# Scores on either pair of TensorE tiles: K and Q kept a second time with exchanged partition halves

## The chip, the cores and the metric

The kernel runs on one core of one Trainium2 chip. Its time is device microseconds of that core; 947.76 us is the median of three runs before the change (947.38 to 948.65). The engines are TensorE (PE; weight loads are listed apart as PEld), VectorE (DVE), ScalarE (ACT), GpSimd (POOL) and SyncE (SP), which issues most transfers.

## The reference

The input x has 224 x 224 positions of 96 channels. Attention is taken in two directions: the first 48 channels of q, k and v in 28 horizontal stripes of 8 rows, the last 48 in 28 vertical stripes of 8 columns. A stripe has 1792 positions.

```python
qkv = jnp.einsum('bhwc,cd->bhwd', x, wqkv)
q, k, v = (qkv[..., :C].copy(), qkv[..., C:2 * C].copy(), qkv[..., 2 * C:].copy())
scale = C2 ** (-0.5)
qh = q[..., :C2].reshape(B * nh, sw * W, C2)
...
ah = _softmax(jnp.einsum('bqc,bkc->bqk', qh, kh) * scale, axis=-1)
oh = jnp.einsum('bqk,bkc->bqc', ah, vh).reshape(B, H, W, C2)
...
o = jnp.pad(oh, ((0, 0), (0, 0), (0, 0), (0, C2))) + jnp.pad(ov, ((0, 0), (0, 0), (0, 0), (C2, 0)))
return jnp.einsum('bhwc,cd->bhwd', o, wo)
```

The vertical stripes (qv, kv, vv, av, ov) go the same way after a transposition of the positions.

## The kernel before

**Stripe pairs.** The 56 stripes are worked on two at a time: 28 stripe pairs P, 14 of horizontal stripes and then 14 of vertical ones. One stripe of a pair lies on partitions 0 to 63, the other on 64 to 127; 48 channels and one extra row are used of each 64. The four 64x64 tiles of TensorE are used as two pairs. The *straight* pair (mode "q" in the code) takes partitions 0 to 63 to output partitions 0 to 63 and 64 to 127 to 64 to 127; the *exchanged* pair (mode "v") takes 0 to 63 to 64 to 127 and the other way round. A *step* is two matmuls, one for each stripe, on the two tiles of one pair; matmuls of the two pairs can run at the same time.

**Units.** The 1792 queries are cut in four chunks (512, 512, 512, 256) and the keys in 28 blocks of 64. A unit is two key blocks (four in the last chunk) by one chunk: two score halves, each one step of 512 columns or two of 256, each into a PSUM bank of its own. There are 984 units for ScalarE and 388 for VectorE and GpSimd.

- A ScalarE unit: two score halves (function qk, line 778; letters "a" in the order), one activation with Exp over both banks (line 824, "A"), two product steps with V (function pv, line 804, "c"), added up in the chunk's bank.
- A VectorE unit computes the exponential through integers: two score halves ("b"), two conversions from PSUM to int16 tiles I (line 844, "j"), then for two units at once two passes that make U and E from I (line 849, "U"; written "u" where VectorE does the pass in place of GpSimd), and three pairs of product steps for I, U and E ("d", "d", "D").

Scores run on the straight pair and products on the exchanged one, because K and Q are stored stripe by stripe and the product's inputs are as the scores left them. For the first four key blocks of a chunk (TURN = 2, "turned" units) it is the other way round. V is stored to match.

**Around the units.** For the next stripe pair, prep() makes K, Q and V by projections from x (lines 535 and 637), with evacuations on VectorE; K's column sums and a small matmul (line 602) take the mean out of Q. x comes by two steps of transfers on SP: blocks() copies two stripes side by side into a scratch array in DRAM (line 411, two transfers), and load() transposes them into SBUF (line 418, two transfers). fin() multiplies a finished chunk with wo (lines 691 and 725), divides by the sums of weights, keeps the horizontal part in Ph_sb and, for vertical stripes, adds both and stores the result (lines 749 and 760; 24 stores on SP for most vertical stripe pairs).

**What sets the order.** Nothing is decided on the chip. Each kind of operation stands in a stream named by a letter. The string SEQ, 11330 letters written out in the file, takes the streams' operations one by one; this fixes the order on every engine, and SP's order of transfers too. The string BANK gives each operation that needs a PSUM bank one of the eight. Work.run() walks both strings, adds to each operation's inputs what last used its bank, and Work.emit() writes waits on semaphores: one counter per engine, and for TensorE one per pair of tiles. An engine runs its list in order, so an operation that waits holds back all behind it.

**Buffers that matter here.** Eight PSUM banks; eight tiles PT for ScalarE's results; NY = 4 sets of I and U and NL = 2 of E; two of K, Q and V, by the parity of P.

Of the kernel before, what the change touches and what calls it, by code (L numbers as in the profile page):

```python
# [6 lines left out]
BF16 = mybir.dt.bfloat16  # L7
# [9 lines left out]
TURN = 2  # L17
# [6 lines left out]
def ndc(P, c):  # L24
# [4 lines left out]
    "HiIxIihIiHiIhiiiihIiHiiihxIiiiIhiIiixhhxhhxxhhihHhxihhHhhhhhexhHhhxefHfxHfeexeaaxefAaxeafAxeaaxcecbAaeaVccjbAa"  # L29
    "acjcbxdAcajacbdAjbcacajxbUAacacjfAeacacfAxuacacbedAjdcacxaeDAbecaceajDbAacjabUcjAbcacajbAajfaUccfAeccaeafAoaaU"  # L30
    "cecAgadradrfdAbdaeDXaDjdbkAfUadjacffAcbeacacXdjbAdakdadjdfddAdceaucacXfcAcaceabdcdADjXafaffbAaeDaDDDjcbAUcacaj"
    "cbcDAcjabaccjcbAaUdaodfDADjadadbedfAdfacjacUcfcbAaedaddfjdAadaegddVdcArcdracacfcAaDeaDUbDDdjbcAacacjcDbcAacjac"
    "UbccDAjabaddocAadaddjcdUbdADdjagaDDDrAcbrcacacjUbcAacacjgccAcraodardbdgAUadjaddbDrAjDagacrcfAcUrcarcacbdAeaDaD"
    "fDjDAbcaceadfdAjdadaddecUdbAdadjafcDcAXXDebacajcbcUAcajcacbccAjcfaadodffAdbkeUadaddgjADbDacarjcbcAacrackcUjbdA"
    "fcacaejdfdAdabeadfdfUAXjcfabacecdAXcdadjabDdDAjbcacaDjfDAcaceUacDccAbaoaDcjbAgadardUjfdfAdfadradDfeADacaeccbVc"
    "fAajcaccbecAacjacUdbdAajdadbdjbddADaDajDdUDAacDcacbcDcAjdbacacjdUbAcajdadbdAodaDaDdjcdAcUdadagcbcArDcracacDcjA"
    "bcUacajgccAraodardbdgAdajUdadfDrAgarDacecfAcacreacUcbAdardadfdjdAbDaDeaDfDAdjacacdecdUAbdadjaDbDcAXXajcacbccAj"
    "bkcaUcacjcccAfadoadfdfAadaedkdbUcgAjcbDaDajcfcAacraecrbcfUcAjdadadebdAadadjdbdcdAXcjaUbaDdjDDAXabaffjDfAcDeacU"
    "accDAbcacjacccbcAoadaUdfjdAagadedffdfAracracDfDAebaUacecfcAcaedajdbdAadjbdadVdcjdAcbDaDjaDbDAdcUjacacbcdAcjaca"
    "cbcDAcjacUabDoAadadjdgddAdcrabraUcdDjdADbaDajDcbcAacjacfcUcAcaecagccAoadrardggUADaraDrddfrAdbrdacacjbcAUacacef"  # L40
    "cDAjDaDaDbecfAcaceacDdjbkdAadkajdDbdAjaUabdddddAXXjcacacbcAcjbacaUcccjcAfadaodfDfAbDaedadUgdjAdbacacrjcbcAaDra"
    "DDfjUDbAadadejdfdAadeaddcdcAXUbacajbdcdAXcDjabaDcjAcbUacacjcfcfAacaccfcbAoaaUcegAdadrajdfdAdraDaDfefdfAUabaecf"
    "ccjAbcacaecfcAcaVjcacbdedAadjbdadjbdAdUDaDajDdDbAcacjacbcdAcjaUcabdcDjbADcadajdAbdaodaUcdcdjcAdadagcbDrADDraca"
    "UcDcjbAcacajccgcAoaadrdbrUdgAdadrajDfDAdragacecfUAcacreaccfdAraddadbedfAdacajcbDADeaDajbkdDdkAcjdaUdaDbDcAXXaj"
    "cacbccAjbcacaUcjcccAfadoadfdfAadaedbdUDfAjDbcacaejcbcAacajcgdbUdArdajdadfrdAaDeaDdbdDAXUDjdabaccjdcAXfafafcbec"
    "DAacUacjcbcDAcajbacccjcAbadUaodfDAdjadadfdfefAaDageUcbcAracraccfjcAacacebcVcfAjadaddbedAadjbdaUDdDjdADbDacjacb"
    "cAdcjacaUcdbDAcajcabDoAdadadjUgdAdDarDarcdcbAcdajbadcDUcAjgaaccrDcrbAacacjccAUaodadbggAjdadadrdbArDaDarcjfUcAc"
    "acradfdedAadacebcfdAdjacacdDeAUbdaDajDbdADdjaDabcDjAXXcbcUacajcfcAcaecacbccAjafakcUofAdfdaaeddbAgdajdaDbDkrcAr"
    "aUcadjfdbdAcaecjadfcAcaceaUcfdfAXfadeabdDDdAXjafaDdbedADacaUjcDcbAcacjacbcDAcjabacccjcUAbaadodfDffAjadaddfedAa"
    "ceacVDbcfAjcacacbecAacUjadbddjbdAagadjdddDAaDrUaDrDbcdAjcaacbccdAcjabaUcDjcDAbacajdbddAjadacUcbocdAdaadjDgDdAc"  # L50
    "argarcDUcDArcarcacbcAccjcadaodbUAaDjaDcfcdgAbedadacrcjbAUdadadrfddAjgaadeddcAdcUarcarbdcAdDjabaDDjAfDaDaeUfcDc"
    "AXXaceacbccAjbacaccjkcccAfkadoaUdffAdaedadgdbArDfarDaccUejbAcacacjbcfdAdjadadbedAacacjbfdfAXcfjabUacDedDAXdadj"
    "abDdDAjDcacUacbcAcDjacaccccAbaoadUdfdjAdfadaedfDfAaDeagcfUcrAbracacedfAdadaeddjbAcVacajcbccAjbacaccjbDUAddaacj"
    "dcDbADaDjacbcdAcjdUcabaoDADajbadgddAjadUaDdrDdrcAbadajdcbcADcjacUagDcArcbrcacaccjAcaadoUdfdAadeadDgbDArdajcacf"
    "UcrAcbdaedadfdAjdadagebDADaDrajbDAcracUacdjcdAbdadjabcDcAXXDjcacaUcbcAacjacfcccecAfaodadbkdfUAgdjadadfrbDAraDa"
    "ceccAakjacUbddfjdbAdacaecjfdAdaceaUcdDdAXbaDajbdDdDAXDjabaDcUjcbAcacajccffAcfcaeacccUAcboaaddfjDAagaDedffAdfUr"
    "dardacfcAeabacecfdAcaVjcacbceAadjbdaddjbAddacacjUdDDAaDbaDcjbcdAacjacbcdcUAjabacDcjDbAadaodcAcjbUadadgjcdADdad"
    "rabrDdcADcjaUgacDrcAbrcacaccjcAaoadUdbdfAjdadadeDgbADacracjUbccAracagjcfdAdardeadfUdAcracaddecdAbacajDdbdDAjaf"
    "aDeDDDAXXbcaucaccAjbcakcakcjcccAfaodaUdfdfADbaeDaddgjAdbDaDarjUDbDAacracfcjcbAcacaejcfcAbadeaUdDdDAXdjabadddjd"
    "cAXdadabucfAcfacjacfcAbecacacjccAcbaoadUdfcAjaDaDbedfAfadjadfUdbAecaaccfjcAcbeacagcjVAdadadbrdfrdAadaDeUdDjdDA"  # L60
    "bcacjaDcbAcdjacacbUccdAjabaccDjDbAadaodDUAdjbadaDdcjdAcgadarbcrdcADUcacjacbcADcjagaccrcAoaUdardbdgAjdadadbrcfA"
    "rDDajcaUgcAaecacfcrDrAbcacadefdAdajdabdedAdUDaDajDdbAdadjabcDcDAXXjcaUcacbcfAcjacacccecAfaodakdbUDfADfjadadebd"
    "AdgaacrcrckcAUajadfdddbeAacajcbdfdAjcacaDdeDUdAXbdDajbaDDcAXDjabadcjcbUAcacjacffAcfcaeacccAbcUoadadfjdAbadaedf"
    "fAdfjaDgaDecbAUacrjaddbdAracacfcjcAacacVefdcbAecadajdbcdUAcjdcacaDbDAaDjbDacdcjdAbUacajcDbDAaodaddjbgAdaUDarDj"
    "dcdAcdardabcDcAjDgacUacrcbrAacacjccbAcoadajUdbAgdajgaddrdAbrDaDarcjfUcAcacracfcAedadadfedAdUadeabdcdcAjdbaDaDj"
    "dDAafabcecAXXjDDDakcakcbucAacacjbcccccAjafUadodfdfAadaedgdbDArDarcaUcfjcbAcacaejcbdfAdjdadadefUdfAabaDdjDdDAXD"
    "faceabcdAXcDUjabaDcdjcbAacjaccfcAacUeaccccbAoadadfjDfAfabeadgdjAbVdadarDjbcAcacracfUcjAcbcacaeDfDAadeadjdbdUAa"
    "dajddcdcdAcacaDbDDcAjbUcacacjDcAdcabaoddAaDajDUgcDcrDAdrabaddcjbcAdadjaUbcdcAjgaaccrcbrAacacoUcAjadadbDfAjDada"
    "dedgUAbdacracjbccAracagjcfdADarDeaUDfDAdradadDedDAbadajcdUbdcAdjabadcjcAXXfcacaecbcAkcjbackacccjcAUfaadodffAad"
    "eaddgbdArDfarDacUcejbcAacacjbcfDAdjabadedUAadadjbfdfAXfjacacdcedcAXabadjcbcdAaDjaDDfcAuacaccDebDUAcacajbccAoad"  # L70
    "adfjfgAfadeaddfdrAVacracDbeDfAcacaedUdjAabdadjbddddAcjacacbcdDuAaDaDdjDbcAUacjacbccDAjacabcDjbAdaUdajdbdAcajca"
    "cbDAodDadadUjcdgcAacragrDcDcAacracrbcUcAjcccadaodbAdajdadgdfDrADragaUdebdAcacrajdbdAcracacfjcAbadeadUdDdDAjdba"
    "DaDjdcAfaafceDUcDAXXcaceacbcAacjacbccjkcccAafkadodfUdfAadaedgdbDArDarcacfjcbUAcadeajdbdfAdjdadacedcAbcacjabdDd"
    "AXDjabUaDdDjfAXcfafabecDAcDacjUaccbcAajcaccccbAoaaddUfjgAdadaedffdfAracracfDDeAbaUcaecfcAceacajcbdAadjbdadVdjb"
# [111 lines left out]
class Work:  # L186
# [29 lines left out]
    def run(s, seq, digits):  # L216
# [4 lines left out]
        for c in seq:  # L221
# [14 lines left out]
            if q != c:  # L236
                op.eng, op.fn = "dve", op.alt
# [697 lines left out]
```

## Time and profile before

| | |
|---|---|
| median of three runs | 947.76 us (947.38 to 948.65) |
| the profiled execution's own time | 947.77 us |
| its span | 945.7 us |
| granted TensorE clock | 0.997 of full |
| TensorE, at least one matmul running | 936.0 us |
| VectorE busy | 881.6 us |
| ScalarE busy | 925.2 us |
| GpSimd busy | 769.2 us |
| bytes moved by DMA | 57.09 MB |

The profile is of one execution. A matmul's end is modelled, and matmuls on different tiles overlap, so TensorE's busy time does not tell how full each pair of tiles is. A row of the timeline gives the start, the length, engine, line and operation, what is written and read, and how many instructions are merged in it. A row of the groups gives the number of instructions, their busy time and mean length, and then the engine's idle time just before them with what ended it. A row of the waits reads: who waited, for whom, the total in us, how often, and the longest. A row of the windows gives the stretch, its length, the busy time and number of instructions of PE, PEld, DVE, ACT and POOL, the clock, the DMA share and GB/s.

### The profile page before, as it was taken

How to read it: one execution, taken by the hardware profiler on the slowest of the kernel's cores; microseconds unless marked ns; L12 is line 12 of the kernel's file. 1: busy time of each engine (PE TensorE's matmuls, PEld its weight loads, DVE VectorE, ACT ScalarE, POOL GpSimd, SP SyncE). 2: the span in 40 equal slices, each digit the busy share in tenths (PEclk: the TensorE clock that was granted, in tenths of full speed). 3: DMA queues.
4: the chain of work that ended last, by engine and by line, in shares of the span. 5: the costliest groups of instructions: out<-in, count | busy, mean ns of one | idle time of the engine just before them, and what ended most of it. 6: DMA issues, size and time to landing. Idle time of an engine off the chain costs nothing.

```text
span 945.7 us, 48281 instructions
## 1 busy us (share of the span) xinstructions
PE 936.0 (99%) x21770; PEld 625.8 (66%) x21770; DVE 881.6 (93%) x1754; ACT 925.2 (98%) x993; POOL 769.2 (81%) x512
## 2 busy tenths in 40 slices
PE   9999999999999999999999999999999999999997
PEld 4666766676776677666666767766666666667664
DVE  8999999999999999999999999999999999999994
ACT  7999999999999999999999999999999999999996
POOL 3778988888886888787898888889879888878883
PEclk9999999999999999999999999999999999999998
DMA  8724513440441343244120515545533534461112
GB/s 141 96 46 72 71 22 53 71 66 9 71 71 22 52 72 47 28 71 71 28 46 10 93 36 81 88 72 86 86 61 67 85 57 81 76 84 30 31 20 44
DMA packets 253254, 57.09 MB, mean 60 GB/s; under 512 B 252936, under 2 KB 252936, under 8 KB 253048
## 3 DMA queue, kind: packets, MB, share of 16 engines
q1 hardware_dynamic: 251464, 53.47, 36.5%
q8 instruction: 170, 2.79, 1.3%
q10 hardware_dynamic: 1584, 0.55, 0.3%
q14 instruction: 36, 0.29, 0.1%
HBM read 19.13 MB, written 28.21 MB: 50 GB/s over the span
## 4 chain that ended last, share of the span: by engine, by line
PE 98%; ACT 1%; DVE 0%; issue 0%
PE ps L804 50%; PE ps L778 36%; PE ps L535 5%; PE ps L637 4%; PE ps L691 1%; PE ps L725 1%; ACT PT L824 1%; PE ps L396 0%; PE ps L602 0%; DVE out_sb L736 0%; PE ps L634 0%; PE ps L496 0%; PE ps L529 0%; DVE OT_sb L870 0%; DVE warm L368 0%
## 5 line engine op out<-in xcount | busy, mean ns | idle before, releaser
L824 ACT ACTIVATE PT<-ps 128x1024 bf16<-128x1024 f32 x984 | 921.2, 1036 | 7.7 <-PE ps L778 3.0
L778 PE MATMUL ps<-QT_sb,KT_sb 49*64 49x512 bf16 (+1 forms) x6272 | 738.8, 354 | 0.7 <-issue 0.6
L844 DVE TENSOR_SCALAR I_sb<-ps 128x512 int16<-128x512 f32 x776 | 511.1, 682 | 21.7 <-PE ps L778 17.2
L804 PE MATMUL ps<-PT,V_sb 64*50 64x512 bf16 (+1 forms) x4496 | 499.4, 350 | 0.2 <-issue 0.2
L778 PEld LDWEIGHTS ps<-QT_sb,KT_sb 49*64 49x64 bf16 x6272 | 282.3, 105 | 159.0 <-ACT PT L824 53.7
L849 POOL TENSOR_SCALAR U_sb<-I_sb 128x2048 int16<-128x2048 int16 x170 | 322.5, 1897 | 55.6 <-DVE I_sb L844 37.0
L849 POOL TENSOR_SCALAR E_sb<-I_sb 128x2048 int16<-128x2048 int16 x164 | 311.1, 1897 | 46.2 <-PE ps L804 18.9
L804 PE MATMUL ps<-U_sb,V_sb 64*50 64x512 bf16 (+1 forms) x1776 | 245.7, 350 | 0.0
L804 PE MATMUL ps<-I_sb,V_sb 64*50 64x512 bf16 (+1 forms) x1776 | 239.7, 352 | 0.2
L804 PEld LDWEIGHTS ps<-PT,V_sb 64*50 64x50 bf16 x4496 | 215.6, 100 | 32.7 <-issue 0.7
L804 PE MATMUL ps<-E_sb,Vs_sb 64*50 64x512 bf16 (+1 forms) x1776 | 233.2, 350 | 0.0
L733 POOL TENSOR_TENSOR out_sb<-tmp,Ph_sb 128x480 bf16<-128x480 f32 (+1 forms) x84 | 85.7, 1028 | 31.0 <-DVE E_sb L849 14.9
L804 PEld LDWEIGHTS ps<-I_sb,V_sb 64*50 64x50 bf16 x1776 | 80.2, 100 | 31.4 <-PE ps L804 8.2
L804 PEld LDWEIGHTS ps<-U_sb,V_sb 64*50 64x50 bf16 x1776 | 89.2, 100 | 14.0
L804 PEld LDWEIGHTS ps<-E_sb,Vs_sb 64*50 64x50 bf16 x1776 | 88.0, 100 | 13.8 <-issue 0.6
L535 PE MATMUL ps<-xa_sb,w_sb 64*64 64x512 bf16 (+3 forms) x440 | 80.2, 356 | 0.2 <-issue 0.2
L870 DVE CAST OT_sb<-ps 128x512 bf16<-128x512 f32 x112 | 68.9, 615 | 9.2 <-PE ps L804 8.5
L535 PE MATMUL ps<-xb_sb,w_sb 64*64 64x512 bf16 (+2 forms) x436 | 77.1, 348 | 0.0
L556 DVE TENSOR_SCALAR_CACHE_REDUCE KT_sb<-ps,bias 128x512 bf16<-128x512 f32 x108 | 72.0, 677 | 1.9 <-PE ps L535 1.5
L549 DVE TENSOR_SCALAR QT_sb<-ps 128x512 bf16<-128x512 f32 (+1 forms) x111 | 67.5, 615 | 3.2 <-PE ps L535 1.8
L637 PE MATMUL ps<-w_sb,xa_sb 64*64 64x48 bf16 x1512 | 65.3, 187 | 0.0
L637 PE MATMUL ps<-w_sb,xb_sb 64*64 64x48 bf16 x1512 | 64.9, 186 | 0.1
(68 smaller groups left out, 604.0 us busy)
## 6 DMA issues: line engine op xcount, KB each, us to landing
x_blocks<-in_x_dram SPq DMA_DIRECT2D x54, 336.0 KB
out_dram<-out_sb SPq DMA_DIRECT2D x104, 42.0 KB
out_dram<-out_sb SPq DMA_DIRECT2D x208, 21.0 KB
out_dram<-out_sb SPq DMA_DIRECT2D x22, 24.0 KB
xa_sb<-x_blocks SPq DMA_TRANSPOSE x27, 5.0
xb_sb<-x_blocks SPq DMA_TRANSPOSE x27, 5.9
Ph_sb<-in_x_dram ACTq DMA_DIRECT2D x1, 336.0 KB, 3.1
out_dram<-out_sb ACTq DMA_DIRECT2D x6, 24.0 KB
```

The lines of the kernel that those rows point to most:

```text
L535: ins = e.matmul(out_, lhsT=wt, rhs=rhs, start=i == 0, stop=startup or i == 1)
L549: return e.tensor_scalar(dst, src, QS if startup else A128, None, ALU.mult)
L556: return e.tensor_scalar(dst, src, bias[:, 0:1], None, ALU.add, ALU.add, accum_out=acc)
L637: ins = e.matmul(out_, lhsT=(xa_sb, xb_sb)[i][b][o:o + 64, 0, t0:t0 + 64], rhs=w2_sb[o:o + 64, i, wblk(P, "v"), 0:C2], start=i == 0, stop= ...
L691: ins = e.matmul(bk3[to:to + 64, s, :], lhsT=OT_sb[b][o:o + CA, blk * 64:(blk + 1) * 64], rhs=wo_sb[0][o:o + CA, :], start=True, stop=True)
L733: return e.tensor_tensor(res, tmp[t][:, 0:n, :], ph, ALU.add)
L778: ins = e.matmul(bank(t.k)[to:to + 64, i * qs:(i + 1) * qs], lhsT=KT_sb[b][64 * w:64 * w + CA, 64 * k:64 * k + 64], rhs=QT_sb[b][64 * w:64 ...
L804: ins = e.matmul(bank(k_.slot.k)[to:to + CP, 0:qs], lhsT=V_[o:o + 64, k, :], rhs=rhs()[o:o + 64, h * 512 + i * qs:h * 512 + (i + 1) * qs], ...
L824: a = wk.add("A", Op("act", ACT, lambda e: e.activation(split(PT[i % NPT]), two(ts), ACTF.Exp, scale=LN128), qs_ + pt_free.get(i - NPT, [] ...
L844: ds.append(wk.add("j", Op("dve", 0.6, lambda e, t=t, at=at: e.tensor_scalar(I_sb[y][:, at:at + 512], bank(t.k), one, 0.0, ALU.add, ALU.ma ...
L849: fn = lambda e, dst=dst, c=c: e.tensor_scalar(dst[:, 0:m], I_sb[y][:, 0:m], float(c), 1.0, ALU.add, ALU.mult)
L870: k.evac = wk.add("o", Op("dve", 0.07 + qs / 960, lambda e, k=k, b=P % 2, q0=q0, qs=qs: e.tensor_copy(OT_sb[b][:, q0:q0 + qs], bank(k.slot ...
```

## The change

K and Q of each stripe pair are copied within SBUF to KS_sb and QS_sb with the two partition halves exchanged, by four transfers on SP (two for K once its last part is evacuated, two for Q). A score half may then be computed by the other pair of tiles, with the copy as its input and the same bank and the same output partitions. The order says so by a letter: "n" in place of "a" and "m" in place of "b". Such a half waits for the last of the four copies of its stripe pair.

With it come: three sets of I and U in place of four (NY), whose room the copies take; a new order and new banks throughout; the projections' matmuls no longer wait for the scores of the stripe pair two before (the evacuations do, by the order's own record of the last scores, and also for the copies' reading); the blocks of stripe pair 2 are loaded after the first copies are issued, and not before stripe pair 0 is prepared; the small transposition of the query weights stands in the first stream of TensorE ("h") and not in "f". The changed expression for `cut` gives the same cuts at TURN = 2.

In the new order 278 of the 1968 score halves of ScalarE units are "n" and 107 of the 776 of VectorE units are "m"; the passes on VectorE ("u") are 64 in place of 54; the copies ("w", and four "x" at the start) are 112. SEQ has 11442 letters; BANK keeps its length.

```diff
@@ Work.run @@
-        vlock = None
+        vlock, last = None, {}
         for c in seq:
-            both, q = c == "p", {"p": "P", "u": "U"}.get(c, c)
+            both, q = c == "p", {"p": "P", "u": "U", "n": "a", "m": "b"}.get(c, c)
             op = s.streams[q][at[q]]
             at[q] += 1
             deps = list(op.deps)
+            if c in "nm":
+                dep, op.mode, op.fn = op.other
+                deps.append(dep)
+            if op.pair is not None:
+                last.setdefault(op.pair, {})[op.mode] = op
+            if op.war is not None:
+                deps += last.get(op.war, {}).values()
...
-    NPT, NY, NL, NR, NT = 8, 4, 2, 4, 3
+    NPT, NY, NL, NR, NT = 8, 3, 2, 4, 3
...
+        QS_sb = [sb(f"QS_sb{i}", [128, NTOK], BF16) for i in range(2)]
+        KS_sb = [sb(f"KS_sb{i}", [128, NTOK], BF16) for i in range(2)]
...
-        blocks(2, "x")
...
@@ prep @@
-            qk_war = list(last_qk[prev2].values()) if prev2 >= 0 else []
+            qk_war = list(last_qk[prev2].values()) + [alt_ready[prev2]] if prev2 >= 0 else []
...
-                              pe_fn, xs + [op_w0] + (mean_ev.get(P, []) if kind == "q" else []) + qk_war, evs, mode="p" if startup else "q", steps=1 if startup else 2)
+                              pe_fn, xs + [op_w0] + (mean_ev.get(P, []) if kind == "q" else []), evs, mode="p" if startup else "q", steps=1 if startup else 2)
                 xt_read[P][p.stream] = p
+                ops[0].war = prev2
...
-                p, ops = fill("f", 0.2, pe_fn, [op_w0, o_id], [("dve", 0.2, lambda e, bk, a=a: cp(e, bk, *a), [o_wq], True, "e")
+                p, ops = fill("h", 0.2, pe_fn, [op_w0, o_id], [("dve", 0.2, lambda e, bk, a=a: cp(e, bk, *a), [o_wq], True, "e")
...
+            war = list(last_qk.get(prev2, {}).values())
+            for dst, src, ready in ((KS_sb[b], KT_sb[b], k_ready[P]), (QS_sb[b], QT_sb[b], q_ready[(P, NCH - 1)])):
+                for w in range(2):
+                    alt_ready[P] = wk.add("w" if P else "x", Op("sp", 0.64, lambda e, dst=dst, src=src, w=w: e.dma_start(dst[64 - 64 * w:128 - 64 * w, :], src[64 * w:64 * w + 64, :]),
+                                                  [ready] + war, lat=3.0, dma=s_alt[b]))
+                    alt_ready[P].war = prev2
...
@@ qk @@
-                def fn(e, t=t, th=th):
-                    for i, k in enumerate(th):
-                        for w in range(2):
-                            to = 64 - 64 * w if turn else 64 * w
-                            ins = e.matmul(bank(t.k)[to:to + 64, i * qs:(i + 1) * qs], lhsT=KT_sb[b][64 * w:64 * w + CA, 64 * k:64 * k + 64],
-                                           rhs=QT_sb[b][64 * w:64 * w + CA, q0:q0 + qs], start=True, stop=True)
-                    return ins
...
+                def score(alt, t=t, th=th):
+                    K_, Q_ = (KS_sb[b], QS_sb[b]) if alt else (KT_sb[b], QT_sb[b])
+
+                    def fn(e):
+                        for i, k in enumerate(th):
+                            for w in range(2):
+                                to = 64 - 64 * w if turn else 64 * w
+                                o = 64 - 64 * w if alt else 64 * w
+                                ins = e.matmul(bank(t.k)[to:to + 64, i * qs:(i + 1) * qs], lhsT=K_[o:o + CA, 64 * k:64 * k + 64],
+                                               rhs=Q_[o:o + CA, q0:q0 + qs], start=True, stop=True)
+                        return ins
+                    return fn
+                o = wk.add(stream, Op("pe", S, score(False), [k_early[P] if kts[-1] < 2 else k_ready[P], q_ready[(P, c)]], steps=len(kts), take=[t],
+                                      book=ts[1:] if pair and not h else [], mode="v" if turn else "q"))
+                o.other, o.pair = (alt_ready[P], "q" if turn else "v", score(True)), P
...
         prep(0, startup=True)
+        blocks(2, "x")
```

More of the change, by code (lines that the diff above doesn't have):

```diff
@@ L34 @@
[L34 to L38, printed above, removed]
@@ L643, in vv @@
                 xs = [x_op[P], op_w2] if not startup else [x_tr] + x_cols(64 * k0, 64 * (k0 + n))
-                cut = [0, n] if startup else [0, 4, 7, n] if k0 == 0 else [n * i // 3 for i in range(4)]
+                cut = [0, n] if startup else [0, 2 * TURN, n] if k0 == 0 and TURN > 2 else [0, 4, 7, n] if k0 == 0 else [n * i // 3 for i in range(4)]
                 part = list(zip(cut[:-1], cut[1:]))
```

277 lines of the change are left out of this document (143 added, 134 removed).

## The prediction

> **What bounds the kernel now.** I read the page's head and its chain of waits first, then ScalarE's own instructions, a short stretch of the timeline, the waits, and two long windows.
>
> ```profile
> span 945.7 us, 48281 instructions
> PE 936.0 (99%) x21770; PEld 625.8 (66%) x21770; DVE 881.6 (93%) x1754; ACT 925.2 (98%) x993; POOL 769.2 (81%) x512
> ...
> PE 98%; ACT 1%; DVE 0%; issue 0%
> ```
>
> The profiled execution took 947.77 us and the median of the runs is 947.76, so a sum made against the one holds for the other; 2.1 us lie outside the span. The chain is matmul throughout, but "PE busy" says only that at least one of the four 64x64 tiles works. Counting from the code, the exchanged pair of tiles has 3848 steps (4296 product steps, less 840 products of turned units, plus 392 turned score steps), the straight pair 3570 (2352 scores, 840 products, 378 for K and Q).
>
> ```profile
> 125.18 3.10 ACT L824 ACTIVATE PT<-ps 128x1024 bf16<-128x1024 f32 x3
> ...
> 126.62 0.38 PE L778 MATMUL ps<-QT_sb,KT_sb 49*64 49x512 bf16 x2
> ...
> 126.64 0.38 PE L804 MATMUL ps<-PT,V_sb 64*50 64x512 bf16 x2
> ...
> 126.84 0.38 PE L778 MATMUL ps<-QT_sb,KT_sb 49*64 49x512 bf16 x2
> ...
> 127.06 0.38 PE L778 MATMUL ps<-QT_sb,KT_sb 49*64 49x512 bf16 x2
> ...
> 127.27 0.38 PE L778 MATMUL ps<-QT_sb,KT_sb 49*64 49x512 bf16 x2
> ```
>
> Steps of one pair follow each other after (127.27 - 126.62)/3 = 0.217 us. So the exchanged pair needs 835 us and the straight one 775 for these steps; V and the output projection bring both to some 840 to 850 of 946. Neither pair is full. What the stretch shows is the order within a unit: two score halves that feed one activation start at 126.62 and 126.84, one behind the other on the same pair, with a product step (126.64) beside them, and the second ends at 127.22. The three activations take 3.10 us; less one duration of 1.02 that is a pace of 1.04 each.
>
> ```profile
> L824 ACT ACTIVATE PT<-ps x984: 1018/1024/1168, 9.7 to 936.5; 128x1024 bf16<-128x1024 f32 x197
> ```
>
> ```profile
> 926.59 11.11 ACT L824 ACTIVATE PT<-ps 128x1024 bf16<-128x1024 f32 x12
> ```
>
> The first row (durations, first and last start) gives 984 activations from 9.7 to 936.5, on average (936.5 - 9.7)/983 = 0.943 us apart. The second is the stretch in which fewest matmuls are left to compete: (11.11 - 1.02)/11 = 0.917 apart. If every activation had that pace the body would be 983 x 0.026 = 25.4 us shorter. That is what late scores cost ScalarE.
>
> ```profile
> PEld ps L778 <- ACT PT L824: 53.7, 218, 0.5
> ...
> PEld ps L778 <- DVE I_sb L844: 21.5, 91, 0.5
> DVE I_sb L844 <- PE ps L778: 17.2, 60, 1.0
> ...
> ACT PT L824 <- PE ps L778: 3.0, 9, 0.9
> ```
>
> The scores wait 218 times for ScalarE to give back a bank, and ScalarE then waits for these scores: a loop through eight banks. It shows as idle time of ScalarE only nine times, because an activation's recorded 1.02 us is longer than the 0.917 at which activations can follow each other.
>
> ```profile
> 40.00:480.00 440.00, 439.26 (x10446) 298.45 (x10440) 411.02 (x810) 436.49 (x468) 366.96 (x221) 1.00 0.35 54
> 480.00:920.00 440.00, 439.90 (x10322) 295.20 (x10314) 424.47 (x837) 437.26 (x468) 372.37 (x260) 1.00 0.38 62
> ```
>
> ```profile
> 840.00:880.00 40.00, 40.00 (x928) 26.17 (x924) 39.16 (x80) 39.70 (x44) 34.47 (x24) 1.00 0.31 45
> ```
>
> After the stretch's length come PE, PEld, DVE, ACT, POOL, the clock, the DMA share and GB/s. VectorE is busy 93% of the first long window and 96% of the second, and 39.16 of 40 us (97.9%) in the last row. It is the second bound. The clock is full.
>
> **The change part by part.** *Split scores.* In the new order I count 278 score halves of ScalarE units and 107 of VectorE units on the other pair; 248 go from straight to exchanged, 137 back, so the exchanged pair gains a net 111 x 0.217 = 24 us (to about 874) and the straight one loses as much. In 268 of the 984 ScalarE units the two halves then stand on different pairs and can start together: the second is ready up to 0.217 us earlier. At 126.84 it would start at 126.62 if no product took its place.
>
> The gain's upper end: 25.4 us, if splits meet every late activation. VectorE caps it. Each long window holds some 467 starts, so ScalarE's excess there is 440 - 467 x 0.917 = 11.8 us. The order moves ten passes from GpSimd to VectorE (54 become 64; six in the first half, four in the second):
>
> ```profile
> L849 POOL TENSOR_SCALAR U_sb<-I_sb 128x2048 int16<-128x2048 int16 x170 | 322.5, 1897 | 55.6 <-DVE I_sb L844 37.0 <-DVE E_sb L849 8.2 <-DVE rc L677 0.4
> ...
> L849 DVE TENSOR_SCALAR U_sb<-I_sb 128x2048 int16<-128x2048 int16 x24 | 17.1, 714 | 0.0
> ```
>
> At 0.714 us each that is 4.3 and 2.8 us more on VectorE (and 1.9 us each off GpSimd, which has idle time). At 97.9% the first window can shrink to (411.0 + 4.3)/0.979 = 424 us, which is below what ScalarE allows, so 11.8 stands; the second to (424.5 + 2.8)/0.979 = 436.4, a gain of 3.6. Upper end 15.4 us. Lower end: were the splits placed at random, they would meet 268/984 = 27% of that, 4.2 us. Nothing in the trace says how well they are aimed; I take the middle, 9.8 us.
>
> *The copies.* Four transfers per stripe pair, 112 in all, each 64 rows of 3584 bytes (224 KB), issued on SP. The trace has no copy within SBUF; the nearest in size and row length (3072 bytes) is the load of 336 KB at the start, which lands after 3.1 us:
>
> ```profile
> Ph_sb<-in_x_dram ACTq DMA_DIRECT2D x1, 336.0 KB, 3.1
> ```
>
> An exchanged score waits for its stripe pair's last copy. From that copy to the first such score the order leaves 4 activations in 4 stripe pairs, 5 in 9, 6 to 9 in 14, at 0.943 us each: 3.8 us at least, so with free queues nothing waits. But in ten stripe pairs of the second half (numbers 16 to 25 from zero) both block loads for a later pair stand on SP just ahead of the copies, one or two activations apart and the second 7 to 9 activations, some 7.5 us, ahead of the first exchanged score. How long such loads fill the queue:
>
> ```profile
> xb_sb<-x_blocks SPq DMA_TRANSPOSE x27, 5.9
> ```
>
> ```profile
> 566.88 3.61 SPq L418 DMA_TRANSPOSE xb_sb<-x_blocks  x1
> 570.53 4.00 SPq L411 DMA_DIRECT2D x_blocks<-in_x_dram  x2
> ```
>
> ```profile
> 572.00:574.00 2.00, 2.00 (x60) 1.82 (x62) 1.89 (x5) 1.97 (x4) 1.92 (x3) 1.00 0.89 182
> ...
> 578.00:580.00 2.00, 2.00 (x40) 1.06 (x36) 2.00 (x6) 2.00 (x3) 1.35 (x1) 1.00 0.61 74
> 580.00:582.00 2.00, 2.00 (x44) 1.58 (x40) 2.00 (x5) 2.00 (x3) 1.92 (x2) 1.00 0.05 8
> ```
>
> The transposition ahead of them lands at about 566.88 + 5.9 = 572.8, so they have the queue from some 572 on; from there to 580 the two loads take 8 us (the last columns are DMA share and GB/s). With the first issued 1.4 us before the second, copies behind both start 6.6 us after the second's issue if the queue serves in order, and land by 6.6 + 3.1 = 9.7. Late by 0 to 2.2 us in ten places: 0 to 22 us, and below nothing it cannot be. I take 0.5 us in each, 5 us, as part of the 3.1 runs beside the load's end. What else stands behind a copy on SP, stores and loads for stripe pairs two and three ahead, is read by nothing soon. The 25 MB more beside 57 MB find a DMA share of 0.35 to 0.38.
>
> *Three I and U buffers instead of four.* The first conversion of a group then waits for the products of the group three before it. Between these two the old order leaves at least 28 PE steps in nine of ten groups, the new one 10 in the middle, 5 or fewer in a quarter and 3 in a tenth. PE makes 10446/2 steps in 440 us, 0.084 us each, so a quarter of the 194 groups (49) has at most 0.42 us, and a product ends 0.38 us after its start. Cost between 0 and 49 x 0.38 = 18.6 us; I take 0.2, since conversions that stand in order behind their product mostly find it done.
>
> *Start-up.* The transposition of the query weights moves forward, the blocks of the third stripe pair behind the first copies:
>
> ```profile
> L618 DVE CAST wqT_sb<-ps 48x128 bf16<-48x128 f32 (+1 forms) x4 | 1.0, 249 | 0.1
> ...
> L614 PE MATMUL ps<-Ph_sb,w_sb 96*48 96x96 bf16 x4 | 0.3, 214 | 0.0
> ```
>
> Between 0 and 1.3 us, if the first activation (9.7) slips by both; I take 0.3, the matmuls alone. The projections no longer wait for old scores (their evacuations do): no gain, that wait was long over.
>
> Sum: 947.8 - 9.8 + 5.0 + 0.2 + 0.3 = 943.5 us.
>
> **The rivals.** *The copies land late (slower).* At their upper end 943.5 - 5 + 22 = 960.5 us; it decides from 0.93 us in each of the ten places, where the net gain of 4.3 is gone. For it: the loads' 8 us and a cover of 6.6 us in the tightest place (7 activations); against it: copies may start on engines that the loads do not fill. What stands behind a waiting score on PE waits with it, and both bounding engines wait for PE. [...]
>
> *The ring of three sets the pace (slower).* At its upper end 943.5 - 0.2 + 18.6 = 962 us; it decides from 4.5 us, that is 0.09 us in each of the 49 tight groups. For it: VectorE has 4% left in the second half; against it: three quarters of the groups have more room, and fewer products in flight also free banks sooner.
>
> *The split changes nothing (same).* The second half on the exchanged pair displaces a product that was there, as at 126.64, and the loop is as long as before: 947.8, within 0.2% (1.9 us, about what a measurement of this kernel can tell from no change). For it: the exchanged pair is the fuller one already. [...]
>
> *All late scores are met (faster).* No cap by VectorE and no late copy: 947.8 - 25.4 + 0.5 = 922.9.
>
> **How the numbers follow.** Forecast (a gain of 2 to 16 us) 0.46, more than that 0.06, nothing 0.11, copies 0.22, ring 0.15. So faster 0.52, same 0.11, slower 0.37. Cases of both signs hold much of the chance: the likeliest one's own range is 932 to 946; the range given leaves out the fastest case and the slow ends of the two slower ones, 931 to 960.
>
> **What would show it.** Right: first to last activation falls from 926.8 us to about 922 us; scores wait for ScalarE well below 53.7 us; VectorE is some 7 us busier. Wrong: scores wait for a transfer into the copies, above all in the second half (copies), VectorE's conversions wait for products (ring), or the first activation starts much after 9.7.

## The result, and the profile after

The changed kernel takes 1022.25 us (median; 1021.47 to 1022.82) beside 948.20 us for the kernel before on the same chip: a ratio of 1.077, with a 95% interval of 1.0759 to 1.0789. The forecast was 943.5 us in a range of 931 to 960. The change makes the kernel 74 us slower.

The first lines of the page of the kernel after: the span, the busy times, the slices, and the chain of waits.

```profile
span 1019.7 us, 48286 instructions
...
PE 959.1 (94%) x21770; PEld 642.5 (63%) x21770; DVE 889.3 (87%) x1764; ACT 926.8 (91%) x993; POOL 751.3 (74%) x502
...
ACT  7999999999999999999996987967978879789995
...
PEclk9999999999999999999998998989989989899998
...
PE 89%; DMA 4%; DVE 4%; issue 1%; ACT 1%; SPq 1%; DVEq 0%
```

No engine has more work than before in any amount near 74 us: VectorE is busy 7.7 us longer (889.3 against 881.6), ScalarE 1.6 us, and TensorE 23.1 us with the same 21770 matmuls (the last section has stretches in which each of them took longer). What is new are holes. Each digit is a fortieth of the span, 25.5 us; after its first slice ScalarE's row is all nines in the first half and falls to 6, 7 or 8 again and again in the second. The chain of waits, which was 98% matmul, now has 4% of waiting for a transfer.

The activations of the kernel after (durations in ns, first and last start in us), cut at 538 us; the first row is the first part of the run, the second the rest.

```profile
L851 ACT ACTIVATE PT<-ps x560: 1017/1025/1117, 9.9 to 537.1; 128x1024 bf16<-128x1024 f32 x187
```

```profile
L851 ACT ACTIVATE PT<-ps x425: 1017/1025/1151, 537.1 to 1008.1; 128x1024 bf16<-128x1024 f32 x142
```

The same two rows of the kernel before:

```profile
L824 ACT ACTIVATE PT<-ps x560: 1018/1024/1119, 9.7 to 537.3; 128x1024 bf16<-128x1024 f32 x187
```

```profile
L824 ACT ACTIVATE PT<-ps x425: 1018/1026/1168, 537.3 to 936.5; 128x1024 bf16<-128x1024 f32 x142
```

The two kernels reach the 560th activation at the same moment, 537.1 and 537.3 us. The other activations take 1008.1 - 537.1 = 471.0 us against 399.2. So the first half has neither gained nor lost, and the whole loss, 71.8 us, lies behind 537 us. The waits of the kernel after (who, for whom, total us, times, longest) say where:

```profile
ACT PT L851 <- PE ps L801: 64.7, 41, 6.7
DVE I_sb L871 <- PE ps L801: 59.7, 76, 7.4
PE ps L801 <- DMA QS_sb<-QT_sb: 47.0, 10, 6.4
PEld ps L801 <- DMA QS_sb<-QT_sb: 45.1, 9, 6.7
PEld ps L801 <- ACT PT L851: 42.2, 182, 0.6
```

TensorE waits ten times for a transfer into QS_sb, the copy of Q, up to 6.4 us at a time; ScalarE and VectorE wait for TensorE. Set beside the kernel before, activation by activation, all of the loss stands in ten places, one in each of the stripe pairs 16 to 25, the very ten in which both block loads stand on SP just ahead of the copies. Each has one gap of 4.6 to 7.7 us between two activations; the gaps make 51.5 us of the loss, and the ten activations behind each gap, mostly the first four, another 20.8. One of the ten places, SP's own timeline (start, duration of the issue, line, operation, count):

```profile
560.37 1.87 SPq L679 DMA_DIRECT2D KS_sb<-KT_sb  x2
562.28 15.66 SPq L779 DMA_DIRECT2D out_dram<-out_sb  x24
577.98 3.55 SPq L423 DMA_DIRECT2D x_blocks<-in_x_dram  x2
581.58 5.40 SPq L679 DMA_DIRECT2D QS_sb<-QT_sb  x2
```

And what VectorE, ScalarE and TensorE do then, from the timeline:

```profile
573.95 1.05 DVE L561 TENSOR_SCALAR QT_sb<-ps 128x512 bf16<-128x512 f32 x2
...
584.62 1.02 ACT L851 ACTIVATE PT<-ps 128x1024 bf16<-128x1024 f32 x1
...
589.53 0.63 PE L801 MATMUL ps<-QS_sb,KS_sb 49*64 49x512 bf16 x2 [4.24 <-DMA QS_sb<-QT_sb]
589.54 0.62 PE L831 MATMUL ps<-PT,V_sb 64*50 64x512 bf16 x2
...
590.26 1.02 ACT L851 ACTIVATE PT<-ps 128x1024 bf16<-128x1024 f32 x1 [4.62 <-PE ps L831]
```

Q is complete at 575.0 us. Its copies could have been issued then, but SP is at that moment in the middle of 24 stores, which it issues from 562.28 to 577.94, and the two block loads come after them. The last copy of Q is through SP at 586.98 us, 12 us after Q was complete. TensorE stands still for 4.24 us in front of the first exchanged score, and the products on the other pair of tiles start together with it, at 589.54. This place is not the pattern of all ten. From the end of Q to the issue of its first copy it is 0.7 to 9.0 us, 5.6 on average, and in stripe pairs 18 and 25 only 1.1 and 0.7. What all ten share is that the first copy behind the second block load takes SP 3.6 to 4.4 us to issue (0.6 is the median of all copies). Counted from the start of the issue, the landing is not long as a rule:

```profile
KS_sb<-KT_sb SPq DMA_DIRECT2D x56, 224.0 KB, 3.4
QS_sb<-QT_sb SPq DMA_DIRECT2D x56, 224.0 KB, 3.7
```

These medians are 3.4 and 3.7 us, where the prediction took 3.1. But in the ten places the first copy behind the loads lands after 6.8 to 7.7 us, most of which is its long issue, and the last copy of Q after 3.6 to 5.1.

### The profile page after: what moved, and what is told of

Read it like the earlier page. It is cut to its first block, busy times and chain, and to the rows that moved or that the text cites. A ratio compares the mean times of both kernels' runs of the same rounds, so it can differ in the third digit from the quotient of the medians.

```text
span 1019.7 us, 48286 instructions
## 1 busy us (share of the span) xinstructions
PE 959.1 (94%) x21770; PEld 642.5 (63%) x21770; DVE 889.3 (87%) x1764; ACT 926.8 (91%) x993; POOL 751.3 (74%) x502
## 4 chain that ended last, share of the span: by engine, by line
PE 89%; DMA 4%; DVE 4%; issue 1%; ACT 1%; SPq 1%; DVEq 0%
PE ps L831 46%; PE ps L801 33%; DMA QS_sb<-QT_sb 4%; PE ps L650 4%; PE ps L547 4%; PE ps L710 1%; DVE I_sb L871 1%; PE ps L744 1%; DVE KT_sb L568 1%; ACT PT L851 1%; SPq L679 1%; DVE tmp L748 1%; PE ps L408 0%; DVE rc L696 0%; PE ps L615 0%
## 5 line engine op out<-in xcount | busy, mean ns | idle before, releaser
L801 PE MATMUL ps<-QT_sb,KT_sb 49*64 49x512 bf16 (+1 forms) x5314 | 697.2, 364 | 1.3 <-DVE KT_sb L568 0.4
L831 PE MATMUL ps<-PT,V_sb 64*50 64x512 bf16 (+1 forms) x4496 | 510.0, 353 | 0.3 <-ACT PT L851 0.3
L801 PEld LDWEIGHTS ps<-QT_sb,KT_sb 49*64 49x64 bf16 x5314 | 253.8, 106 | 131.1 <-ACT PT L851 42.2
L876 POOL TENSOR_SCALAR E_sb<-I_sb 128x2048 int16<-128x2048 int16 x153 | 290.7, 1900 | 46.9 <-PE ps L831 20.3
L831 PE MATMUL ps<-U_sb,V_sb 64*50 64x512 bf16 (+1 forms) x1776 | 252.1, 355 | 0.0
L831 PEld LDWEIGHTS ps<-PT,V_sb 64*50 64x50 bf16 x4496 | 221.2, 101 | 43.0 <-issue 5.3
L831 PE MATMUL ps<-I_sb,V_sb 64*50 64x512 bf16 (+1 forms) x1776 | 247.5, 362 | 0.6 <-issue 0.5
L801 PE MATMUL ps<-QS_sb,KS_sb 49*64 49x512 bf16 (+1 forms) x958 | 144.0, 349 | 47.3 <-DMA QS_sb<-QT_sb 47.0
L752 POOL TENSOR_TENSOR out_sb<-tmp,Ph_sb 128x480 bf16<-128x480 f32 (+1 forms) x84 | 85.7, 1029 | 60.9 <-DVE E_sb L876 29.7
L831 PEld LDWEIGHTS ps<-I_sb,V_sb 64*50 64x50 bf16 x1776 | 85.1, 102 | 36.1 <-PE ps L831 12.0
L831 PEld LDWEIGHTS ps<-U_sb,V_sb 64*50 64x50 bf16 x1776 | 91.7, 101 | 17.4 <-issue 3.0
L801 PEld LDWEIGHTS ps<-QS_sb,KS_sb 49*64 49x64 bf16 x958 | 48.5, 106 | 58.1 <-DMA QS_sb<-QT_sb 45.1
```

Source lines behind the costliest of these rows:

```text
L752: return e.tensor_tensor(res, tmp[t][:, 0:n, :], ph, ALU.add)
L801: ins = e.matmul(bank(t.k)[to:to + 64, i * qs:(i + 1) * qs], lhsT=K_[o:o + CA, 64 * k:64 * k + 64], rhs=Q_[o:o + CA, q0:q0 + qs], start=Tr ...
L831: ins = e.matmul(bank(k_.slot.k)[to:to + CP, 0:qs], lhsT=V_[o:o + 64, k, :], rhs=rhs()[o:o + 64, h * 512 + i * qs:h * 512 + (i + 1) * qs], ...
L876: fn = lambda e, dst=dst, c=c: e.tensor_scalar(dst[:, 0:m], I_sb[y][:, 0:m], float(c), 1.0, ALU.add, ALU.mult)
```

## The experiments

Five theories stood against each other: the block loads fill the transfer queue, so that the copies land late (the prediction's rival); SP itself is late, because stores, loads and waits stand ahead of the copies in its list; the copies' bytes or their issue cost time everywhere; the ring of three costs time; and, for the gain that did not come, that a split is worth nothing or that it is badly aimed.

In most experiments only SP's part of the order is changed. Written for the stripe pairs 16, 17 and 18, with T for a transposition, B for a block load, y24 for the 24 stores and w for a copy (two for K, then two for Q), the kernel after has

```
16: T T y24 B B w w w w
17: T T w w y24 B B w w
18: T T w y24 B w B w w
```

and so on to stripe pair 25.

**Block loads behind the copies.**

```diff
-16: T T y24 B B w w w w
-17: T T w w y24 B B w w
-18: T T w y24 B w B w w
+16: T T y24 w w w w B B
+17: T T w w y24 w w B B
+18: T T w y24 w w w B B
```

> The changed kernel, with one edit of the order: in the ten places of the second half the two block loads stand on SP just behind the four copies, and not just ahead of them. Theory 1 (queue): the copies were late because they stood behind the loads; the scores' wait for the copies (47 + 45 us in the changed kernel's waits) falls to almost nothing and the time to 945 to 952 us. Rival A (the new order or the ring of three is slow by itself, and the wait only shows where it would have waited anyway): still 1000 us or more, with another wait in its place. Rival B (too many bytes for the transfer engines): the copies stay late or the block loads become late; 980 us or more.

Measured: 970.19 us, ratio 1.024 (1.0218 to 1.0263). Most of the loss goes, not all. Waits of this kernel:

```profile
PEld ps L801 <- DMA QS_sb<-QT_sb: 14.6, 6, 3.9
PE ps L801 <- DMA QS_sb<-QT_sb: 14.2, 7, 3.6
```

SP's timeline at one of the stalls that are left:

```profile
608.06 3.97 SPq L423 DMA_DIRECT2D x_blocks<-in_x_dram  x2
618.97 1.35 SPq L430 DMA_TRANSPOSE xa_sb<-x_blocks  x1
...
622.47 16.33 SPq L779 DMA_DIRECT2D out_dram<-out_sb  x24
638.92 1.95 SPq L679 DMA_DIRECT2D KS_sb<-KT_sb  x2
640.91 1.23 SPq L679 DMA_DIRECT2D QS_sb<-QT_sb  x2
```

No block load stands near these copies, and Q was complete at 635.6 us, yet they are issued from 640.91 on: the 24 stores ahead of them run until 638.80. The loads, now later, also hold back the transposition that needs them, which waits 6.9 us for them, and with it the stores. So the queue of transfers is not the whole cause; SP's own list is part of it.

**No split scores, copies still made.** Every "n" becomes "a" and every "m" "b".

```diff
-     "AanocmceAgdadarDfrDAdaeUdadjbdwAcacajcwbccAajafdbkfkfjAdaXdfaedUdmAcaedacdjcdADfnXDaDefDfAanucfcmcDAeancDXcdjc"
+     "AaaocbceAgdadarDfrDAdaeUdadjbdwAcacajcwbccAajafdbkfkfjAdaXdfaedUdbAcaedacdjcdADfaXDaDefDfAaaucfcbcDAeaacDXcdjc"
...
```

> The changed kernel with every score half on its own pair of tiles again (n read as a, m as b); copies, ring of three and the order of all else as changed. Nothing waits for a copy any more. Theory 1: the ten long waits go, so about 950 us, and whatever the split was worth shows as the distance to the run with the loads behind the copies (if it was worth 5 us or more, this one is at 955 or more). Rival A: 1000 us or more. Rival B: about 950 too, since nobody reads the copies.

Measured: 987.28 us, ratio 1.0419 (1.0404 to 1.0435). Nothing waits for a copy any more, but all is slower, from the start. Its activations up to 538 us:

```profile
L851 ACT ACTIVATE PT<-ps x540: 1017/1024/1105, 9.9 to 537.8; 128x1024 bf16<-128x1024 f32 x180
```

540 activations where the kernels before and after have 560: 3.6% fewer. The new order without its splits is slower than the old order, so it was laid out for the splits and needs them.

**No split scores, and the block loads behind the copies**: both edits together.

```diff
-16: T T y24 B B w w w w
+16: T T y24 w w w w B B
...
-     "AanocmceAgdadarDfrDAdaeUdadjbdwAcacajcwbccAajafdbkfkfjAdaXdfaedUdmAcaedacdjcdADfnXDaDefDfAanucfcmcDAeancDXcdjc"
+     "AaaocbceAgdadarDfrDAdaeUdadjbdwAcacajcwbccAajafdbkfkfjAdaXdfaedUdbAcaedacdjcdADfaXDaDefDfAaaucfcbcDAeaacDXcdjc"
...
```

> Both edits: loads behind the copies, and no score half exchanged. Beside the run with the loads moved alone it prices the split itself in the same order and with no late copy. If the split shortens the scores' loop as predicted: 5 to 15 us slower than the run with the split. If the split is worth nothing: within 2 us of it. Against the run without splits alone: within 2 us, if the loads' place matters only through the copies.

Measured: 985.84 us, ratio 1.0403 (1.0386 to 1.0421), the same as with the loads ahead (987.28). So the place of the loads costs nothing by itself here; it costs through the scores that read the copies. Beside the kernel with splits and the loads behind (970.19), the splits are worth 985.84 - 970.19 = 15.7 us even with the stalls that it still has.

**Block loads issued by ScalarE.** From stripe pair 18 on blocks() issues on ScalarE's queue.

```diff
-                ops.append(wk.add(stream, Op("sp", 1.4, lambda e, dst=dst, src=src: e.dma_start(dst, src), [], lat=7.0, dma=s_xs[P % 4])))
+                ops.append(wk.add(stream, Op("act" if P >= 18 else "sp", 1.4, lambda e, dst=dst, src=src: e.dma_start(dst, src), [], lat=7.0, dma=s_xs[P % 4])))
```

> The changed kernel with the same order, but the block loads of stripe pairs 18 to 27 are issued by ScalarE's queue, so that they are in no queue ahead of the copies, at the same time as before. Theory 1 in its strict form (order within SP's own queue): the copies land in 3 to 5 us and the waits of 5 to 7 us shrink to below 2; time 950 to 975 us, as 20 issues on ScalarE cost it up to 0.7 us each. Theory 1 in a looser form (the loads fill the transfer engines whatever the queue): the waits stay at half or more of what they were, 985 us or more.

Measured: 976.19 us, ratio 1.0305 (1.0283 to 1.0327). The loads still run beside the copies (in stripe pair 17 ScalarE issues them from 570.70 to 575.33 us, and SP the copies of Q from 571.35 on); only SP is relieved of them. The waits for the copies shrink from 47.0 and 45.1 us to 3.8 and 5.5:

```profile
PEld ps L801 <- ACT PT L851: 66.5, 206, 3.4
...
PEld ps L801 <- DMA QS_sb<-QT_sb: 5.5, 5, 1.3
...
PE ps L801 <- DMA QS_sb<-QT_sb: 3.8, 5, 1.0
```

The loss moved to ScalarE, which now spends its own time on the issue (its timeline):

```profile
570.70 4.63 ACTq L423 DMA_DIRECT2D x_blocks<-in_x_dram  x2
...
575.43 1.94 ACT L851 ACTIVATE PT<-ps 128x1024 bf16<-128x1024 f32 x2 [2.80 <-issue]
```

Beside loads that another engine issues, a copy of Q lands after 3.9 us in the median and 7.9 at most, and TensorE waits for it five times, 1.0 us at most. ScalarE's own stops put the scores off as well and may hide part of that. In both runs the issue of the loads held up the engine that did it: the two took SP 3.55 us at 577.98 in the kernel after, and ScalarE 4.63 us at 570.70 here, far more than the 0.7 each that were expected.

**Copies first: loads and stores both behind them.**

```diff
-16: T T y24 B B w w w w
-17: T T w w y24 B B w w
-18: T T w y24 B w B w w
+16: T T w w w w B B y24
+17: T T w w w w B B y24
+18: T T w w w w B B y24
```

> The changed kernel with both the block loads and the 24 stores that stand on SP ahead of the copies moved behind them, in the ten places. Theory 1, mended (SP is one queue in order: first the loads' landing, then the stores' 16 us of issue, hold the copies back): with both out of the way no score waits for a copy by more than 1 us, and the time is 945 to 950 us, as the first half of the changed kernel runs exactly at the old pace. Rival B (transfer engines full): copies still land late, 960 us or more. Rival C (VectorE or the order limits the second half even so): 952 to 965 us with no wait for copies.

Measured: 993.20 us, ratio 1.0478 (1.0457 to 1.0498), worse than with the loads alone behind and far from the 945 to 950 expected. One wait for a copy is left, of 7.8 us, and a new one is there:

```profile
POOL out_sb L752 <- DMA out_dram<-out_sb: 44.4, 9, 7.5
```

The stores now come behind the loads, so late that GpSimd finds out_sb still unread when it wants to write the next results, nine times and up to 7.5 us long. So the stores have a deadline too.

**Only the stores behind the copies.**

```diff
-16: T T y24 B B w w w w
-17: T T w w y24 B B w w
-18: T T w y24 B w B w w
+16: T T B B w w w w y24
+17: T T w w B B w w y24
+18: T T w B w B w w y24
```

> The changed kernel with only the 24 stores moved behind the copies; the block loads stay ahead of them. If the loads alone hold the copies (prediction's term): the ten waits stay at 4 us or more, 990 us or more. If the stores' issue on SP is what makes the copies late: 955 to 975 us.

Measured: 957.33 us, ratio 1.0102 (1.0085 to 1.0118). The block loads stand ahead of the copies just as in the kernel after, and none of the ten stalls is left. There is one new one, in stripe pair 26, which the edit did not touch (SP's timeline, then a row of ScalarE's):

```profile
834.72 16.50 SPq L779 DMA_DIRECT2D out_dram<-out_sb  x24
...
855.06 16.08 SPq L779 DMA_DIRECT2D out_dram<-out_sb  x24
871.26 1.17 SPq L679 DMA_DIRECT2D KS_sb<-KT_sb  x2
872.47 1.28 SPq L679 DMA_DIRECT2D QS_sb<-QT_sb  x2
```

```profile
877.95 1.02 ACT L851 ACTIVATE PT<-ps 128x1024 bf16<-128x1024 f32 x1 [7.05 <-PE ps L831]
```

The displaced stores of stripe pair 25 push that pair's own stores back, which still stand ahead of its copies; no block load is there at all, and ScalarE loses 7.05 us. Stores alone make such a stall.

**The stores behind the copies in stripe pairs 26 and 27 as well.**

```diff
-26: T T y24 w w w w
-27: w y24 w w w
+26: T T w w w w y24
+27: w w w w y24
```

> The changed kernel with the stores moved behind the copies in twelve stripe pairs: the ten of the run before (957.3 us) and the last two, whose copies that run made late instead (8.1 us at activation 913, and 2.4 after it). Theory 1 in its mended form: no score waits for a copy by more than 1 us; 957.3 - 9.9 = 947.4 us, or 946 to 948.5, that is, the same as the kernel before or faster by up to 0.2%. The prediction's term for the split (9.8 us) would want 938 to 940. If the stores moved back hold the end: 950 us or more, with the last activation on time and the end late.

Measured: 949.08 us beside 948.53, ratio 1.0006 (0.9997 to 1.0015): no difference. All of the loss is undone by an order of SP's list, with the splits, the copies, the block loads ahead of them and the ring of three kept. Its copies land as before, in 3.5 us (median). This is also the fair measure of the split, since nothing disturbs it; below it is called the undisturbed order. Its profiled execution is the shortest of the eleven, 946.03 us. Two long windows (stretch, length, busy us and count of PE, PEld, DVE, ACT, POOL, clock, DMA share, GB/s):

```profile
40.00:480.00 440.00, 439.25 (x10436) 302.61 (x10436) 412.92 (x818) 437.13 (x469) 354.29 (x214) 1.00 0.47 81
480.00:920.00 440.00, 439.57 (x10368) 295.91 (x10364) 427.34 (x844) 437.12 (x469) 368.57 (x258) 1.00 0.51 90
```

469 activations start in each, where the kernel before has 468. One activation in 440 us is 0.2%.

**Block loads early: ahead of the stores.**

```diff
-16: T T y24 B B w w w w
-17: T T w w y24 B B w w
-18: T T w y24 B w B w w
+16: T T B B y24 w w w w
+17: T T w w B B y24 w w
+18: T T w B B y24 w w w
```

> The changed kernel with the two block loads moved ahead of the 24 stores in the ten places; between these loads and the Q copies SP then issues the stores for some 16 us, and what it issues before the copies is the same in number. If the copies are late because the loads fill the transfer queue just then (a Q copy took SP up to 4.4 us to issue, and landed after up to 7.7): the loads are through by then, the waits fall below 2 us each, 948 to 965 us. If SP's own time for all that stands ahead of the copies is what makes them late: the waits stay at 4 us or more, 990 us or more.

Measured: 985.07 us, ratio 1.0397 (1.0375 to 1.042). The loads are issued some 20 us before the copies of Q here, so they are out of the transfer engines' way, and still TensorE waits for the copy in six of the ten places, 2.5 to 5.2 us each. One of them (SP's timeline and the score that waited):

```profile
592.45 3.95 SPq L423 DMA_DIRECT2D x_blocks<-in_x_dram  x2
596.44 20.30 SPq L779 DMA_DIRECT2D out_dram<-out_sb  x24
...
617.36 1.97 SPq L679 DMA_DIRECT2D QS_sb<-QT_sb  x2
```

```profile
622.38 0.64 PE L801 MATMUL ps<-QS_sb,KS_sb 49*64 49x512 bf16 x2 [5.04 <-DMA QS_sb<-QT_sb]
```

Q was complete at 611.6 us, within the 20.3 us of stores. So stores alone, with no load near, make the copies late. The time lies between the two that were expected, though: with the loads no longer just ahead of the copies, half of the loss is gone (1022 to 985 us). Neither of the first two theories is enough by itself. All that stands on SP ahead of the copies adds up, as in the kernel after: the stores (15.66 us at 562.28), the loads (3.55 us at 577.98), and the long issue of the first copy behind the loads (3.6 to 4.4 us). The stores are the longest part, and the one whose removal alone ends the ten stalls.

**No copies at all.** Without splits and without KS_sb and QS_sb (the order as in "No split scores", without the letters of the copies):

```diff
-            for dst, src, ready in ((KS_sb[b], KT_sb[b], k_ready[P]), (QS_sb[b], QT_sb[b], q_ready[(P, NCH - 1)])):
-                for w in range(2):
...
-                    alt_ready[P].war = prev2
+            alt_ready[P] = q_ready[(P, NCH - 1)]
```

> The changed kernel without exchanged halves and without the copies themselves (no transfers into KS and QS, no such tiles), ring of three. Against the run without exchanged halves but with the copies (987.3 us): within 3 us if the copies cost nothing but the waits for them; 5 us or more faster if their 25 MB or their waits on SP cost something by themselves.

Measured: 987.00 us, ratio 1.0419 (1.0403 to 1.0434), beside 987.28 with the copies made and not read. The copies' 25 MB cost nothing that these runs could tell.

**No copies, ring of four.**

```diff
-    NPT, NY, NL, NR, NT = 8, 3, 2, 4, 3
+    NPT, NY, NL, NR, NT = 8, 4, 2, 4, 3
```

> The same, with four sets of I and U in place of three, in the same order. If the ring of three is what makes this order need the split (rival of the prediction): 950 to 970 us. If it is the order itself, which sets scores later because it counts on two halves at once: within 4 us of the run with three sets.

Measured: 986.56 us, ratio 1.0413 (1.0397 to 1.0428). In this order a fourth set of I and U is worth 0.4 us, within the spread of the runs.

**More splits.** In the order with all stores behind the copies, 84 more late ScalarE units have one half on the other pair of tiles (82 of them move to the exchanged pair).

```diff
-DDjbADwkdadkajcwdbdA
+DDjbADwkdadknjcwdbdA
...
```

> The same, with 84 more ScalarE units split: those that in the run with the stores moved were late by over 100 ns although both halves stood on one pair, and whose copies are there (14.7 us of lateness in all; 82 go from straight to exchanged, 18 us of steps). If lateness is the serial halves' own doing, as the prediction has it: 4 to 10 us faster than the run without them. If the exchanged pair, now some 95% full, or what stands behind in the order takes the place of it: within 2 us, or slower.

Measured: 961.35 us, ratio 1.0137 (1.0123 to 1.0151), slower by 12 us. ScalarE's wait for scores:

```profile
ACT PT L851 <- PE ps L801: 15.0, 55, 0.9
```

Without the additional splits it is

```profile
ACT PT L851 <- PE ps L801: 4.6, 10, 0.9
```

The prediction's picture, that a late activation is helped when its halves may start together, would have made this faster. It made ScalarE wait 55 times instead of 10. The exchanged pair now has 82 x 0.217 = 18 us more work. Against a pace of 0.917 us, the 352 units that are now split are late by 29.7 us in all, and the same units by 17.4 without the additional splits; the other units are late by 7.5 and 5.9. Whether it is that pair's fill or the products pushed back in TensorE's list that does it, these runs don't tell.

## Why the prediction was wrong

**The copies: right place, wrong size by a factor of 14.** This is the step that failed: "late by 0 to 2.2 us in ten places", 0.5 us taken in each, 5 us in all. Measured are the ten places named, stripe pairs 16 to 25, and 71.8 us of loss in them, 7.2 us each, three times the upper bound.

Two parts of the step held. TensorE came to the first exchanged score 5.4 to 9.4 us after the issue of the second load, 7.35 on average, where the step has some 7.5. And the first copy behind that load landed 8.0 to 10.7 us after the load's issue, where the step has 9.7. What failed is that the step lets the copies behind the loads start all together, so that 9.7 is the landing of all of them. SP issues them one after another, the first holds it for 3.6 to 4.4 us, and an exchanged score waits for the last of four. The last one landed 8.8 to 14.0 us after the issue of the second load, 12.0 on average, and 13.1 to 14.0 where all four copies stand behind the loads. So TensorE waited 3.1 to 6.4 us, 4.7 on average, and not 0.5. The price failed too: a wait was taken at its own length, and 4.7 us of it cost 7.2 (the last section says why).

The step's row of the kernel before, 4.00 us for the issue of two loads, has the time that SP stands there; the step used it for the transfers alone. Its sentence on "what else stands behind a copy on SP" does not ask what stands *ahead*: 24 stores at 15.66/24 = 0.65 us of issue each. The copies came late in the order as it stands, with the second load issued about where the order has it; but with the stores out of the way ("Only the stores behind the copies") SP issues the second load 11 us or more ahead of the first exchanged score, and none of the ten stalls is left.

**The split's gain: 9.8 us predicted, nothing measured.** The bounds were 4.2 and 15.4. Up to 537 us, where no stall disturbs it, the change gains 0.2 us; in the order without stalls, 1.0006 (0.9997 to 1.0015). What failed here is the share of the difference between two paces, 0.943 and 0.917, that splits can win (25.4 us in all). Counted activation by activation against the pace of 0.917, only 7.0 of these 25.4 us of the kernel before stand at the 268 units that the new order splits. In the profiled execution of the undisturbed order these are late by 4.3 us, and the other units by 18.9 in place of 18.5. So the splits met 28% of the lateness, about the 27% of the prediction's lower end, for splits placed at random, and took 2.7 us of it in this execution; of that the medians show nothing. There was also the unspoken footing that the new order differs from the old one only in the splits. It doesn't: with its splits taken out it is slower than before (987.28), and inside it the splits are worth 987 - 949 = 38 us. It sets the two halves of a split unit next to each other: they are 1.1 scores and products apart in TensorE's list, and 1.9 in the units of the old order. On one pair of tiles two such halves started one behind the other, at 126.62 and 126.84 us in the kernel before. Why the new order without splits loses so much more than the old one is not shown beyond that. Of the prediction's own signs one misled: scores were to wait for ScalarE "well below 53.7 us", and they do (42.2 us, and 44.9 in the undisturbed order), with no gain in time. The splits in the old order were not tried.

**The rivals.** "The copies land late" is what happened, beyond its upper end of 960.5 us. Of what was said with it, that what stands behind a waiting score on TensorE waits with it holds: after the wait of 4.24 us the score on the one pair and the product on the other start again together, at 589.53 and 589.54 us. "The ring of three sets the pace" is out: without splits four sets give 986.56 beside 987.00, and with splits, in the undisturbed order, VectorE's conversions wait for products 3.1 us in all (0.2 in the kernel before). "The split changes nothing" is right in its time for the undisturbed order. Its reason is left open: in the new order taking all splits out costs 38 us, and 84 more of them cost 12.

**What held.** The first activation starts at 9.9 us (9.7 before; 0.3 more was predicted). VectorE is busy 7.7 us longer (7.1 predicted). The copies' bytes cost nothing that the runs could tell. The sign named for being wrong, scores that wait for a transfer into the copies, above all in the second half, is just what the waits show.

One count of the prediction is off by four: the turned units have 836 product steps, not 840, as the first chunk has no VectorE unit. That moves 4 x 0.217 = 0.9 us between the pairs and decides nothing.

The two profiled executions differ by 1021.47 - 947.77 = 73.7 us. The last activation starts 1008.1 - 936.5 = 71.6 us later, and what follows it in the span takes 11.6 us in place of 9.2.

## What to carry to other kernels

When a transfer that somebody soon waits for is put on a queue, add up the issue times of everything *ahead* of it there, and the waits of that, from when its input is complete; several transfers are issued one after another (here the first copy behind the loads held SP for 3.6 to 4.4 us), and the last one's landing counts (here 8.8 to 14.0 us after the issue of the second load). The transfers' own lengths come after that. A queue that never mattered has no slack on record: it can run late with no trace of a wait (here a copy left it up to 12 us after its data were there) until the first transfer with a deadline stands in it. And when a hand-made order is replaced along with the mechanism, the mechanism's gain can't be read from the old order's idle times: the new order may behave differently without it.

## What the runs showed of the hardware

**Each of the ten stalls of TensorE came with a lower clock too.** Windows of the kernel after, one with a stall and the next without:

```profile
540.00:560.00 20.00, 14.18 (x248) 8.57 (x242) 11.30 (x25) 11.25 (x12) 9.48 (x7) 0.83 0.57 109
560.00:580.00 20.00, 20.00 (x500) 13.00 (x496) 19.36 (x37) 19.95 (x23) 17.02 (x13) 1.00 0.32 63
```

The granted clock is 0.83 over the 20 us with the stall and 1.00 in the next. In the trace's record of the granted clock it is 1.00 up to 548.6 us and 0.50 from there to 555.4. It falls to 0.50 around the end of every one of the ten stalls, seven times for 6.8 us and three times for 3.4, and right after a stall the matmuls take 0.63 us (589.53) in place of 0.38. In the seven places the ten activations behind the gap lose 2.0 to 3.0 us, in the three 1.0 to 1.4, and this goes with the clock and not with the length of the stall: stalls of 3.45 and 3.52 us are among the seven, stalls of 3.96 and 4.24 among the three. So a place costs 5.15 us in its gap and 2.1 behind it, which is how waits of 4.7 us on average (47.0/10) come with a loss of 7.2. The ten gaps of TensorE are 3.11 to 6.42 us long.

**The issue of one copy held SP for up to 4.37 us.** All issues of copies of Q in the kernel after, in ns, and their landing:

```profile
L679 SPq DMA_DIRECT2D QS_sb<-QT_sb x56: 461/597/4367, 18.0 to 971.8; - x56
...
DMA to landing us min/median/max: 2.8/3.7/7.7
```

An issue of a copy took 0.6 us in the median, and 3.6 to 4.37 us for the first copy behind block loads in the ten places; with the block loads some 20 us earlier ("Block loads early") the longest was 1.88 us. When ScalarE issued the loads, it stood still for 2.80 us itself. Whether a full queue is the reason, these traces don't show.
